# Spectral mixing and a SwiGLU block on one core: the head of the first batch rearranged

## The chip, the core and the metric

The kernel runs on one core of a Trainium2 chip. The core has five engines that follow instruction streams of their own: TensorE (PE in the profile, with PEld for its weight loads), VectorE (DVE), ScalarE (ACT), GpSimd (POOL) and SyncE (SP), which here only issues DMA transfers. The metric is the device time of one execution in microseconds.

## The reference

For each of 8 batches the input x (3008 tokens by 256 channels, float32) is filtered in the frequency domain along the tokens, and the result goes through a SwiGLU block whose weights come as float64:

```python
X = np.fft.rfft(x, axis=1)
F = (filt_r + 1j * filt_i)[None, :, :]
y = np.fft.irfft(X * F, n=x.shape[1], axis=1).astype(np.float32)
x = y.reshape(B * S, D)                      # 24064 x 256
g = x @ w_gate                               # w_gate, w_val: 256 x 1536
silu = g * (1.0 / (1.0 + np.exp(-g)))
out = (silu * (x @ w_val) @ w_out).astype(np.float32)   # w_out: 1536 x 256
```

## The kernel before

**Spectral part.** 3008 = 47 x 64, and the transform is taken in two factors, as matrix products with tables of cosines and sines. `stage1` transforms over 47, `stage2a` over 64 (24 frequencies s in 12 pieces u of two, `N_TWO`); VectorE multiplies by the filter, GpSimd adds the two parts of the complex product, and `stage2b` transforms back over 64. `stage3` transforms back over 47 and leaves the tokens as matrix y. Between `stage2b` and `stage3` the data go through HBM (`d2`, tile d in the profile), since the partitions must be regrouped. `stage3` works on four chunks k of 8 of the first 32 positions; each chunk needs 96 rows (24 frequencies x 4), of four positions in each of two pieces i. `load_t4` reads these rows back.

**Block part.** A step is one chunk k with one third g of the hidden width. `SCHEDULE` is an order, written out by hand, of tokens for all engines: Q and P are products with y, A, B and E are products of sums of y (tile y_t, `combine_sequence`) with sums of weights, which save multiplications; f and c are copies of a product's bank by ScalarE, x and y combine two banks on VectorE, D is a difference on GpSimd, h is the gated product, S are sums of h on GpSimd, W are the products with w_out (banks wF, wA, wG). A bank's later product waits until earlier readers have done: P1 follows f1, P0 follows f0.

**Weights.** They come as float64 and are turned into float32 by the kernel, in 36 halves of 128 x 256 values. `round_half(i)` is a generator that does one half in small instructions: mantissa bits (L403), exponent bits (L406), mantissa to float (L408), exponent with its bias taken off and clamped (VectorE L412 and L415 for i < 8, ScalarE L419, L421, L423 for later ones), sign and exponent joined (L426), low word added (L430), and GpSimd multiplies the two (L438, or L450 and L451). Halves 0 to 7 are w_val and w_gate for g = 0; 8 to 11 are w_out for it, of which four halves make the two sets j = 0 and 1, each finished by four differences on GpSimd (L329). `combine_weights` makes the sums of weights for one pair of blocks: A on VectorE, for some pairs a scaling on ScalarE (L472), then B and E.

**The planner.** `Preparation` gives each of these small instructions a tick, and `tick(step, n)` issues the next n ticks at that place of the program. A half begins 4 ticks after the one before it, but half 8 begins 12 ticks after half 7. `finish(step)` issues what the step needs. In the first step 11 ticks come at places of `SCHEDULE` after A01, in later ones 20.

**The head.** Before the first step the kernel runs batch 0's spectral part by itself, in a loop over u in which `stage2b` trails `stage2a` by `lag` pieces; matmuls named idle, on a tile of zeros or on weights, stand in its gaps. `stage2b`'s result goes from its bank by a ScalarE copy into one of four buffers g and by DMA to `d2`; piece u + 4 needs the buffer of u, so its copy waits until that store has landed. Pieces 0 to 7 are stored by SP's queue, 8 to 11 by ScalarE's. The rows of chunk 0 go into the tile f0, in two loads for each half i; those of the last piece do not go through HBM: eight small transfers bring them straight from g to f0 (L923). The instructions of each engine keep the order of the program (`pin`), so a waiting one holds up all behind it on its engine.

The sums of the weights for g = 0 end with B on GpSimd, and E on VectorE for four of the six pairs.

Of the kernel before, what the change touches and what calls it, by code (L numbers as in the profile page):

```python
# [48 lines left out]
B, S, C = 8, 3008, 256  # L49
# [5 lines left out]
NS, NQ = 24, 64  # L55
NR = 2 * N1
NK = 4 * NS
# [67 lines left out]
def dft_tables():  # L125
# [26 lines left out]
    d[0, :, :, 1] = (-sn * sg).transpose(0, 2, 1)  # L152
    d[1, :, :, 1] = (c * sg).transpose(0, 2, 1)
    d = d.reshape(128, NS, 128)
    de = np.stack([d, d.transpose(2, 1, 0)], 2)

    hi = 2 * np.pi * (np.outer(2 * n1 + 1, s) % (2 * N1)) / (2 * N1)
    scale = np.where(s == 0, 1.0, 2.0) / S
# [45 lines left out]
def kernel(  # L204
# [168 lines left out]
        return spot if i < N_LENT and spot < 3 else None  # L373

    N_EARLY = 12

    def load_weights(i):
        if i in raws or i >= len(weights):
# [9 lines left out]
    def round_half(i):  # L388
# [19 lines left out]
        pin(nc.scalar.activation(out=w, in_=man, func=AF.Copy, scale=2.0 ** -20, bias=1.0))  # L408
        yield
        pf = pw.bitcast(FP32)  # L410
        if i < 2 * len(BLOCKS):
            pin(v.tensor_scalar(out=pf, in0=pw, scalar1=-896.0, scalar2=0.0,  # L412
                                op0=ALU.add, op1=ALU.max))
            yield
            pin(v.tensor_scalar(out=pw, in0=pf, scalar1=255.0, scalar2=2.0 ** 23,  # L415
                                op0=ALU.min, op1=ALU.mult))
            yield
        else:
            pin(nc.scalar.activation(out=pf, in_=pw, func=AF.Relu, bias=off_t))  # L419
            yield  # L420
            pin(nc.scalar.activation(out=pf, in_=pf, func=AF.Relu, bias=top_t, scale=-1.0))  # L421
            yield
            pin(nc.scalar.activation(out=pw, in_=pf, func=AF.Copy, scale=-(2.0 ** 23),  # L423
                                     bias=255 * 2.0 ** 23))
            yield
# [34 lines left out]
    def combine_weights(g, i, j):  # L460

        d = j - i
        wt_f = weights_of(0, 0, g).rearrange("p s z f -> p s (z f)")
        m = wt_f[:, SLOT[f"A{i}{j}"]]
        ui, uj, yi, yj = [wt_f[:, SLOT[f"{p}{q}"]] for p in "PQ" for q in (i, j)]
        if d == 1:
            pin(negated_sum(m, ui, uj))
        else:
            pin(add(nc.vector, m, ui, uj))
        yield  # L470
        if d > 1:
            pin(nc.scalar.mul(m, m, -1.0 / d))  # L472
        yield
        pin(sub(nc.gpsimd, wt_f[:, SLOT[f"B{i}{j}"]], yi, m))
        early = g == 0 and PAIRS_USED.index((i, j)) < 4
        pin(add(nc.vector if early else nc.gpsimd, wt_f[:, SLOT[f"E{i}{j}"]], yj, m))

    def keep_weights(g, piece):

# [7 lines left out]
    class Preparation:  # L487
# [3 lines left out]
        def __init__(self):  # L491
            self.at, self.held = 0, []

            self.ticks, self.need = {}, {}
            base, ready = [], {}

            def put(t, f, by, pool=False):
                self.ticks.setdefault(t, ([], []))[pool].append(f)
                self.need[by] = max(self.need.get(by, 0), t)

            for i, (_, (use, *at)) in enumerate(weights):
                hid, g = use == "hid", at[0] if use == "hid" else at[0] // JB
                by = ((0, 3, 6) if hid else (1, 4, 7))[g]
                b = base[-1] + (4 if i != 2 * len(BLOCKS) else 12) if i else 0
                if i >= N_EARLY:
                    same = [n for n in range(N_EARLY, i) if spot_of(n) == spot_of(i)]
                    k = 2 if spot_of(i) is None else 1
                    last = base[same[-k]] + 8 if same[k - 1:] else 0
                    b = max(b, last + 8)
                    put(max(last, b - 10), lambda i=i: load_weights(i), by)  # L510
                base.append(b)
                if hid and g == NG - 1:
                    ready.setdefault(NT, b)
                half = []
# [6 lines left out]
                times = (0, 1, 2, 3, 4, 6, 7, 9, 10) if i >= 2 * len(BLOCKS) else \  # L521
                    (0, 1, 2, 3, 4, 6, 9, 10)
                for t in times:
                    put(b + t, go, by, t > 8 or t == 7)
                if hid and at[1:] == [BLOCKS[-1], 1]:
                    for n, pair in enumerate(PAIRS_USED):
                        c = combine_weights(g, *pair)
                        for t in range(3):

                            put(b + 11 + n + t, lambda c=c: next(c, None),  # L530
                                by if g or n < 4 else 1, t == 2)
            self.barriers = sorted((t, step) for step, t in ready.items())
            self.end = max(self.ticks)
# [57 lines left out]
    class Spectral:  # L591


        def __init__(self, b):
            self.b = b
            self.d1, self.d2 = [dram_tiles[2 * (b % 2) + i] for i in range(2)]
            self.d1_rows = self.d1.rearrange("a (h n) c -> (a h) n c", h=2)

            self.d2_tokens = self.d2.rearrange("a n c -> (a n) c").rearrange(
                "(n a) c -> n a c", n=N2)  # L600
            self.d2_rows = self.d2.rearrange("a (h n) c -> (a h) n c", h=2)
# [51 lines left out]
        def load_tables(self, i):  # L653
# [5 lines left out]
            for u in range(i * n // NV, (i + 1) * n // NV):  # L659
                self.tb[u], self.f[u] = tb0[:, ts(u, NV)], f0[:, ts(u, NV)]  # L660

        def load_t4(self, k, i, part=None):
            if part is not None:

                t = f0[0:NK, ts(i, NH), :]
                r = (slice(0, 64), slice(64, NK - 4 * NV))[part]
                self.load(out=t[r], in_=self.d2_rows[r, ts(i, NH), :])
            else:
                t = t4pool.tile([128, NH, C], FP32, name=f"t4_{self.b}_{k}_{i}", tag="t4")
                at = 2 * k + i  # L670
                if self.b == 0:
                    self.load(out=t[0:NK], in_=self.d2_rows[:, ts(at, NH), :])
                else:

                    rows = self.d2_tokens.rearrange("(h n) a c -> h (n a) c", h=2)
# [233 lines left out]
        def stage2b(self, u):  # L909
# [8 lines left out]
            if self.b == 0 and u == N_TWO - 1:  # L918
                for i in range(NV):
                    pin(nc.scalar.copy(out=g[:, i], in_=ps[:, i]))  # L920
                for j in range(4 * NV):
                    i, at = j // 4, 64 * (j // 2 % 2) + 32 * (j % 2)
                    pin((nc.scalar, nc.sync)[j % 2].dma_start(  # L923
                        out=f0[4 * NV * u + j:4 * NV * u + j + 1, 0:2 * NH],
                        in_=g[at:at + 2 * NH, i:i + 1]))
            else:
                pin(nc.scalar.copy(out=g, in_=ps))
            queue = nc.scalar if self.b or u >= 8 else nc.sync
            if self.b == 0:
                pin(queue.dma_start(out=self.twos(self.d2, u), in_=g))  # L930
                return
            rows = self.d2_tokens.rearrange("n (p s) c -> (n p) (s c)", p=2)
            pin(queue.dma_start(out=rows[:, ts(u, NV * C)], in_=g.rearrange("q s c -> q (s c)")))
# [243 lines left out]
    with tc.tile_pool(name="start", bufs=1) as spool0:  # L1177
# [45 lines left out]
        idle(zero, [bank("idle") for _ in range(2)], 512)  # L1223
        preparation.tick(0, 5)
        spec.real_part(0)
        lag = 4
        for u in range(N_TWO + lag):
            if u < N_TWO:
                spec.turn(u + 2)
# [16 lines left out]
                for i in range(8, N_EARLY):  # L1246
                    load_weights(i)
            if u == N_TWO - 1:
                for i in range(2):
                    spec.load_t4(0, i, 0)  # L1250
        for i in range(2):
            spec.load_t4(0, i, 1)
        for i in range(2):
            spec.load_t4(1, i)
        preparation.finish(0)
        preparation.tick(0, 4)

        idle(zero, [bank("idle") for _ in range(4)], 512)
        for p in ("A13", "A01"):
# [6 lines left out]
            following.load_x(u)  # L1266
    for d in (2, 1):
        combine_sequence(spec.y[0], d, va=nc.vector)

    def keep_y(k):  # L1270
        pin(nc.sync.dma_start(out=y_dram[k], in_=cur.y[k]))
# [207 lines left out]
```

## Time and profile before

| | |
|---|---|
| time, median of 3 runs | 2827.3 us (2824.12 to 2830.31) |
| span of the profiled execution | 2826.7 us |
| granted TensorE clock, mean | 0.998 |
| PE busy in 60 to 80 us | 13.74 of 20 us |
| PE busy in 80 to 100 us | 18.97 of 20 us |
| PE busy in 100 to 120 us | 17.92 of 20 us |
| PE busy in 120 to 140 us | 20.00 of 20 us |
| POOL busy in 100 to 120 us | 19.69 of 20 us |

A view by windows gives each engine's busy time in a stretch. A view by waits tells what ended an engine's idle time. Between 28 and 100 us its longest entries are these (engine, line waited at, what ended it: us in total, times, longest):

```profile
POOL wt_t L329 <- ACT wt_t L472: 8.6, 1, 8.6
DVE wt_t L326 <- ACT wt_t L472: 6.0, 1, 6.0
ACT wt_t L472 <- DMA f<-x: 4.6, 1, 4.6
ACT x L927 <- DMA d<-x: 4.5, 4, 2.4
```

The first three are one wait seen from three engines: GpSimd and VectorE want a scaled sum of weights, ScalarE has still to make it, and it stands behind the small transfers f<-x that ScalarE's queue issues. The fourth is the wait for a free buffer g.

A few names of tiles: wpb and wpc are the banks of `stage2a` and `stage2b`, wpd those of `stage3` for chunk 0 (pd for later chunks), wk the banks of P and Q, wa and we those of A and B, E, wt_t holds the weights of the hidden part, wo_t those of w_out, pw and w are a half in work.

### The profile page before, as it was taken

The page shows a single profiled execution, that of the slowest core. Times are in us where ns is not written, and L with a number is a line of the kernel's source. Part 1 is how long each engine was busy: PE and PEld are TensorE (multiplying, and loading weights), DVE is VectorE, ACT ScalarE, POOL GpSimd, SP SyncE. Part 2 cuts the span into 40 slices and gives each one's busy share as a digit, 9 for nine tenths or more (in the row PEclk, how much of TensorE's full clock was granted, in tenths as well). Part 3 has the DMA queues.
Part 4 walks back from the last instruction along what each step waited for, and adds up shares of the span by engine and source line. Part 5 has one row for each costly group of instructions (what it writes and reads, how often), then busy time and mean ns, then how long its engine had stood idle before and what let it go on. Part 6 is the DMA issues. An engine that isn't in the chain of part 4 may idle for free.

```text
span 2826.7 us, 48513 instructions
## 1 busy us (share of the span) xinstructions
PE 2786.0 (99%) x15444; PEld 2318.8 (82%) x15444; DVE 1993.1 (71%) x4567; ACT 1564.5 (55%) x4182; POOL 1578.1 (56%) x1683
## 2 busy tenths in 40 slices
PE   8999999999999999999999999999999999999998
PEld 6877878788888888888888888888888888888887
DVE  7898766767667766677766677667676767666666
ACT  5775445555555555555555555555555555555554
POOL 4886575465545654456644566444665455545544
PEclk9999999999999999999999999999999999999999
DMA  9687866877666776667666676667766777654543
GB/s 238 210 275 248 274 215 213 281 221 235 192 184 203 246 221 180 198 212 237 218 185 197 214 242 205 186 192 233 230 207 178 217 222 226 194 149 151 152 137 82
DMA packets 363477, 586.59 MB, mean 208 GB/s; under 512 B 198444, under 2 KB 246380, under 8 KB 363128
## 3 DMA queue, kind: packets, MB, share of 16 engines
q1 hardware_dynamic: 337962, 534.70, 60.9%
q10 hardware_dynamic: 23470, 45.46, 5.9%
q0 software_dynamic: 1792, 3.34, 0.4%
q8 instruction: 125, 2.05, 0.3%
q14 instruction: 128, 1.05, 0.1%
HBM read 467.81 MB, written 101.34 MB: 201 GB/s over the span
## 4 chain that ended last, share of the span: by engine, by line
PE 88%; POOL 3%; DVE 1%; issue 1%; DMA 1%; ACT 0%; ACTq 0%; SPq 0%; POOLq 0%; DVEq 0%
PE wa L1050 24%; PE wk L1050 16%; PE wA L1147 16%; PE we L1050 12%; PE wG L1147 8%; PE wF L1147 4%; PE pd L953 3%; PE wqa L700 2%; PE wqc L759 1%; PE wqb L771 1%; POOL out_dram L1132 1%; POOL h L329 1%; POOL y_t L326 0%; DMA lent<-later_tbl 0%; POOL h L326 0%
## 5 line engine op out<-in xcount | busy, mean ns | idle before, releaser
L1050 PE MATMUL wa<-y_t,wt_t 128*128 128x188 f32 x4464 | 879.5, 323 | 6.1 <-DMA y_t<-yt 1.9
L1050 PEld LDWEIGHTS wa<-y_t,wt_t 128*128 128x128 f32 x4464 | 747.2, 190 | 83.1 <-ACT wa L1076 10.8
L1050 PEld LDWEIGHTS wk<-y,wt_t 128*128 128x128 f32 x2976 | 496.6, 191 | 110.8 <-issue 33.4
L1050 PE MATMUL wk<-y,wt_t 128*128 128x188 f32 x2976 | 573.5, 326 | 5.0 <-DVE y L326 2.8
L326 POOL TENSOR_TENSOR h<-h 128x376 f32<-128x376 f32 x190 | 183.3, 986 | 694.5 <-DVE h L1097 694.5
L329 POOL TENSOR_TENSOR h<-h 128x376 f32<-128x376 f32 x572 | 558.8, 998 | 15.4 <-DVE h L326 15.2
L1147 PE MATMUL wA<-h,wo_t 128*128 128x376 f32 x1532 | 552.3, 483 | 3.6 <-DVE o L326 3.5
L1050 PE MATMUL we<-y_t,wt_t 128*128 128x188 f32 x2232 | 431.8, 323 | 0.7 <-ACT we L1081 0.7
L329 POOL TENSOR_TENSOR D<-f,f 128x376 f32<-128x376 f32 x288 | 279.8, 986 | 258.6 <-ACT f L1065 258.5
L329 DVE TENSOR_TENSOR we<-we,m 128x376 f32<-128x376 f32 x576 | 319.4, 555 | 136.5 <-PE we L1050 70.1
L1050 PEld LDWEIGHTS we<-y_t,wt_t 128*128 128x128 f32 x2232 | 369.5, 190 | 1.5 <-ACT we L1081 1.2
L1147 PEld LDWEIGHTS wA<-h,wo_t 128*128 128x128 f32 x1532 | 275.5, 190 | 113.3 <-issue 6.2
L1085 ACT COPY m<-wa 128x376 f32<-128x376 f32 x576 | 272.6, 473 | 103.0 <-PE wa L1050 100.2
L333 DVE SCALAR_TENSOR_TENSOR y<-wk,c 128x376 f32<-128x376 f32 x480 | 244.4, 539 | 61.4 <-ACT c L1069 39.0
L1092 ACT ACTIVATE g<-wa 128x188 f32<-128x188 f32 x576 | 187.6, 326 | 165.8 <-PE wa L1050 155.3
L1092 ACT ACTIVATE u<-we 128x188 f32<-128x188 f32 x576 | 188.2, 327 | 160.1 <-DVE we L329 153.3
L1147 PE MATMUL wG<-h,wo_t 128*128 128x376 f32 x768 | 274.0, 479 | 0.0
L1069 ACT COPY c<-wk 128x376 f32<-128x376 f32 x288 | 136.4, 473 | 224.8 <-PE wk L1050 189.2
L1065 ACT ACTIVATE f<-wk 128x376 f32<-128x376 f32 x288 | 140.4, 488 | 171.1 <-PE wk L1050 124.3
L1081 ACT COPY we<-y 128x376 f32<-128x376 f32 x480 | 222.2, 480 | 19.6 <-DVE h L1097 13.9
L1097 DVE TENSOR_TENSOR h<-wa,g 128x188 f32<-128x188 f32 x576 | 198.5, 345 | 37.1 <-ACT g L1092 36.8
L1097 DVE TENSOR_TENSOR h<-we,u 128x188 f32<-128x188 f32 x576 | 197.5, 344 | 26.6 <-ACT u L1092 15.6
(165 smaller groups left out, 3515.5 us busy)
## 6 DMA issues: line engine op xcount, KB each, us to landing
wt_t<-w_all SPq DMA_DIRECT2D x174, 896.0 KB
wt_t<-w_all SPq DMA_DIRECT2D x174, 768.0 KB
lent<-filter SPq DMA_DIRECT2D x36, 1024.0 KB
lent<-d SPq DMA_DIRECT2D x84, 256.0 KB
d<-lent ACTq DMA_DIRECT2D x84, 256.0 KB
d<-lent ACTq DMA_DIRECT2D x96, 192.0 KB
lent<-raw SPq DMA_DIRECT2D x144, 128.0 KB
t<-d SPq DMA_DIRECT2D x112, 128.0 KB
```

Of the source, the lines that this page charges most:

```text
L326: return eng.tensor_tensor(out=dst, in0=a, in1=b, op=ALU.add)
L329: return eng.tensor_tensor(out=dst, in0=a, in1=b, op=ALU.subtract)
L333: return nc.vector.scalar_tensor_tensor(out=dst, in0=a, scalar=-1.0, in1=b, op0=ALU.mult, op1=ALU.subtract)
L953: pin(nc.tensor.matmul(out=rows, lhsT=self.t4[k, i][:, j, ts(cb, 128)], rhs=cols, start=j == 0, stop=True, skip_group_check=True))
L1050: pin(nc.tensor.matmul(out=ps[:, z], lhsT=self.wt[:, SLOT[p], z], rhs=rhs, start=start and z == 0, stop=True, skip_group_check=True))
L1065: pin(act.mul(self.small(f"f{i}", f"f{i}", 1), t[f"k{i}"], -1.0))
L1069: pin(act.copy(out=self.small(f"c{i}", f"c{i}", 1), in_=t[f"k{i}"]))
L1081: pin(act.copy(out=self.bank(f"e{at}"), in_=t[f"y{at}"]))
L1085: pin(act.copy(out=self.small(f"m{at}", "m", 4), in_=t[f"a{at}"]))
L1092: pin(act.activation(out=self.small(op, "g", 3, 1)[:, 0], in_=ps[:, 1], func=AF.Silu))
L1097: pin(v.tensor_tensor(out=dst, in0=ps[:, 0], in1=g, op=ALU.mult))
L1147: pin(nc.tensor.matmul(out=self.tiles[at], lhsT=wo_t[:, JB * q + i, WO[p], :], rhs=self.hs[i][:, HID[p]], start=start and i == 0, stop=Tru ...
```

## The change

It concerns batch 0 alone, and there what comes before and in the first step. Six edits:

- the columns of the table for `stage2b` are permuted, so that its rows come out in the order of the chunks, 32 rows for each chunk;
- pieces 8 to 11 are therefore stored in two parts: the 32 rows of chunk 0 at once, by ScalarE's queue, the other 96 (`rest`) by SP's after chunk 0 has been read. The eight direct transfers are dropped; chunk 0 is now read in two loads, of frequencies 0 to 15 and 16 to 23;
- `lag` is 3 instead of 4;
- halves 5, 6 and 7 have their exponents done by ScalarE (`N_SHORT` = 5);
- B and E of all six pairs for g = 0 are on VectorE;
- half 8 begins 20 ticks after half 7 instead of 12, the last two pairs' sums come 3 ticks later, and instead of 4 ticks ahead of `stage3` of chunk 0 there are 10 ticks after the sums of y.

They are to shorten the way from the last piece to the first product with weights, and to take work off GpSimd there.

```diff
-    de = np.stack([d, d.transpose(2, 1, 0)], 2)
+    chunks = np.arange(128).reshape(2, 2, NCHUNK, NW).transpose(2, 0, 1, 3).ravel()
+    de = np.stack([d, d.transpose(2, 1, 0)[:, :, chunks]], 2)
...
+    N_SHORT = 5
...
-        if i < 2 * len(BLOCKS):
+        if i < N_SHORT:
             pin(v.tensor_scalar(out=pf, in0=pw, scalar1=-896.0, scalar2=0.0,
                                 op0=ALU.add, op1=ALU.max))
...
-        pin(sub(nc.gpsimd, wt_f[:, SLOT[f"B{i}{j}"]], yi, m))
-        early = g == 0 and PAIRS_USED.index((i, j)) < 4
-        pin(add(nc.vector if early else nc.gpsimd, wt_f[:, SLOT[f"E{i}{j}"]], yj, m))
+        e = nc.gpsimd if g else nc.vector
+        pin(sub(e, wt_f[:, SLOT[f"B{i}{j}"]], yi, m))
+        pin(add(e, wt_f[:, SLOT[f"E{i}{j}"]], yj, m))
...
-                b = base[-1] + (4 if i != 2 * len(BLOCKS) else 12) if i else 0
+                b = base[-1] + (4 if i != 2 * len(BLOCKS) else 20) if i else 0
...
-                            put(b + 11 + n + t, lambda c=c: next(c, None),
+                            put(b + 11 + n + t + 3 * (n > 3 and not g), lambda c=c: next(c, None),
...
+        def rows(self, t, k, s, n):
+
+            self.load(out=t.rearrange("p (o n) c -> p o (n c)", o=1),
+                      in_=self.d2_rows[k, s, :, n].rearrange("s a n c -> s a (n c)"))
+
         def load_t4(self, k, i, part=None):
             if part is not None:
 
-                t = f0[0:NK, ts(i, NH), :]
-                r = (slice(0, 64), slice(64, NK - 4 * NV))[part]
-                self.load(out=t[r], in_=self.d2_rows[r, ts(i, NH), :])
+                a, e = ((0, 16), (16, NS))[part]
+                self.rows(f0[4 * a:4 * e, 0:NW], k, slice(a, e), slice(0, NW))
...
             if self.b == 0 and u == N_TWO - 1:
                 for i in range(NV):
                     pin(nc.scalar.copy(out=g[:, i], in_=ps[:, i]))
-                for j in range(4 * NV):
-                    i, at = j // 4, 64 * (j // 2 % 2) + 32 * (j % 2)
-                    pin((nc.scalar, nc.sync)[j % 2].dma_start(
-                        out=f0[4 * NV * u + j:4 * NV * u + j + 1, 0:2 * NH],
-                        in_=g[at:at + 2 * NH, i:i + 1]))
...
-                pin(queue.dma_start(out=self.twos(self.d2, u), in_=g))
+                q = 128 if u < 8 else 4 * NW
+                pin(queue.dma_start(out=self.d2_parts[0:q, ts(u, NV)], in_=g[0:q]))
+                if q < 128:
+                    self.rest.append((u, g))
...
-        lag = 4
+        lag = 3
...
             if u == N_TWO - 1:
-                for i in range(2):
-                    spec.load_t4(0, i, 0)
-        for i in range(2):
-            spec.load_t4(0, i, 1)
+                spec.load_t4(0, 0, 0)
+        spec.load_t4(0, 0, 1)
+        for u, g in spec.rest:
+            spec.load(out=spec.d2_parts[4 * NW:, ts(u, NV)], in_=g[4 * NW:])
         for i in range(2):
             spec.load_t4(1, i)
         preparation.finish(0)
-        preparation.tick(0, 4)
...
     for d in (2, 1):
         combine_sequence(spec.y[0], d, va=nc.vector)
+    preparation.tick(0, 10)
```

More of the change, by code (lines that the diff above doesn't have):

```diff
@@ L519, in go @@
                     next(half[0], None)
-                times = (0, 1, 2, 3, 4, 6, 7, 9, 10) if i >= 2 * len(BLOCKS) else \
+                times = (0, 1, 2, 3, 4, 6, 7, 9, 10) if i >= N_SHORT else \
                     (0, 1, 2, 3, 4, 6, 9, 10)
@@ L600, in __init__ @@
                 "(n a) c -> n a c", n=N2)
-            self.d2_rows = self.d2.rearrange("a (h n) c -> (a h) n c", h=2)
+            flat = self.d2.rearrange("a n c -> (a n) c")
+            self.d2_parts = flat.rearrange("(s q) c -> q s c", q=128)
+            self.d2_rows = flat.rearrange("(s k a n) c -> k s a n c", k=NCHUNK, a=4, n=NW)
+            self.rest = []
             self.x, self.t2, self.f, self.tb, self.p, self.t4, self.y = {}, {}, {}, {}, {}, {}, {}
@@ L660, in load_tables @@
                 self.tb[u], self.f[u] = tb0[:, ts(u, NV)], f0[:, ts(u, NV)]
+        def rows(self, t, k, s, n):
+            self.load(out=t.rearrange("p (o n) c -> p o (n c)", o=1),
+                      in_=self.d2_rows[k, s, :, n].rearrange("s a n c -> s a (n c)"))
         def load_t4(self, k, i, part=None):
             if part is not None:
-                t = f0[0:NK, ts(i, NH), :]
-                r = (slice(0, 64), slice(64, NK - 4 * NV))[part]
-                self.load(out=t[r], in_=self.d2_rows[r, ts(i, NH), :])
+                a, e = ((0, 16), (16, NS))[part]
+                self.rows(f0[4 * a:4 * e, 0:NW], k, slice(a, e), slice(0, NW))
+                for i in range(2):
+                    self.t4[k, i] = f0[0:NK, ts(i, NH), :]
+                return
             else:
@@ L671, in load_t4 @@
                 if self.b == 0:
-                    self.load(out=t[0:NK], in_=self.d2_rows[:, ts(at, NH), :])
+                    self.rows(t[0:NK], k, slice(0, NS), ts(i, NH))
                 else:
```

## The prediction, made before the changed kernel had run

> **What bounds the kernel now.** I read the page first. TensorE carries the span, so elsewhere an edit counts only where it moves TensorE; the DVE, ACT and POOL shares are averages.
>
> ```profile
> PE 2786.0 (99%) x15444; PEld 2318.8 (82%) x15444; DVE 1993.1 (71%) x4567; ACT 1564.5 (55%) x4182; POOL 1578.1 (56%) x1683
> ```
>
> The edits all lie before the second step of batch 0, so next I read busy time in windows of 2 us. Columns: busy us of PE, PEld, DVE, ACT, POOL; clock; DMA share; GB/s. TensorE stands idle at 65 to 67 and 74 to 76, and then runs at half clock.
>
> ```profile
> 64.00:66.00 2.00, 0.61 (x2) 0.00 (x0) 0.00 (x0) 0.00 (x0) 0.00 (x0) 1.00 0.78 247
> 74.00:76.00 2.00, 0.00 (x0) 0.00 (x0) 1.35 (x4) 1.42 (x4) 0.33 (x1) 0.99 0.82 190
> 76.00:78.00 2.00, 1.18 (x4) 1.18 (x5) 1.44 (x5) 1.89 (x6) 0.00 (x0) 0.50 0.03 9
> 82.00:84.00 2.00, 2.00 (x12) 1.89 (x11) 1.01 (x2) 0.54 (x2) 2.00 (x2) 0.80 1.03 399
> ```
>
> Then the timeline (start, duration, instruction, idle before and its releaser) tells why.
>
> ```profile
> 62.05 4.17 ACTq L923 DMA_DIRECT2D f<-x  x4
> 66.94 0.42 ACT L472 ACTIVATE wt_t<-wt_t 128x256 f32<-128x256 f32 x1 [4.64 <-DMA f<-x]
> 67.40 0.81 SPq L606 DMA_DIRECT2D f<-d  x2
> 70.21 3.78 PE L956 MATMUL wpd<-wi_t,f 96*128 96x94 f32 x32 [0.63 <-PE widle L588]
> 74.52 0.51 ACT L419 ACTIVATE pw<-pw,off_t 128x256 f32<-128x256 uint32 x1 [1.12 <-DVE pw L406]
> 75.92 0.83 ACT L968 COPY y<-wpd 128x376 f32<-128x376 f32 x2
> 78.22 2.29 POOL L326 TENSOR_TENSOR y_t<-y_t 128x376 f32<-128x376 f32 x2 [3.89 <-DVE y_t L326]
> 81.44 0.48 ACT L1065 ACTIVATE f<-wk 128x376 f32<-128x376 f32 x1 [0.83 <-PE wk L1050]
> 83.91 0.88 PE L1050 MATMUL wa<-y_t,wt_t 128*128 128x188 f32 x4
> ```
>
> The last rows of chunk 0 reach SBUF for the product at 70.21. Its results are evicted only at 75.92: ACT is in order, and eleven weight instructions stand ahead, the last of them waiting for DVE. The second factor (f1, done at 81.92) frees the bank for P1 and P0, and A13 follows at 83.91.
>
> [...] the 128x256 weight addition takes 0.42 with POOL idle and 0.95 beside it, and a 0.41 us instruction waited out a POOL sum.
>
> ```profile
> 59.91 0.42 DVE L326 TENSOR_TENSOR wt_t<-wt_t 128x256 f32<-128x256 f32 x1
> 68.60 0.95 DVE L326 TENSOR_TENSOR wt_t<-wt_t 128x256 f32<-128x256 f32 x1
> 96.64 0.98 POOL L326 TENSOR_TENSOR y_t<-y 128x376 f32<-128x376 f32 x1 [2.38 <-PE we L1050]
> 96.69 1.21 DVE L430 SCALAR_TENSOR_TENSOR w<-wo_t,w 128x256 f32<-128x256 uint32 x1
> ```
>
> [...] Here 2.8 us of idling (74.0 to 76.8) sufficed once, and about 6.8 us at half followed (76.8 to about 83.6, from the clock column).
>
> [...]
>
> **Part by part.**
>
> *Halves 5 to 7 on ScalarE.* DVE loses six instructions at 26.1 to 32.6 (about 2.8 us as they stand), ACT gains nine of about 0.5. DVE can start the spectral multiplies up to 1 us before 32.96, its floor being the copy on POOL (30.96 + 1.47). On the path: nothing. The tail is paced by ACT's evictions, each behind the landing of an earlier store (58.38 waits for a DMA), and the loads ahead of these stay.
>
> *Trail of three.* One more store goes ahead of the 1 MB of w_out loads, one trailing product fewer is left at the end. ACT from 58.38 needs four copies of about 0.6 and three issues of 0.38: 62.3 before, I take 62.0. Hidden behind those landings otherwise.
>
> *Rows by chunks, split stores.* The eight direct copies (62.05 to 67.3 on two queues) go. Instead: a 64 KB store, the load behind it. The last full store, issued at about 58.1, let its reader issue at 60.90, 2.8 later for 256 KB; I take 2.4 from issue for a quarter: 64.4. The old last load took 2.8 from the first of two issues to the product; one issue is 0.4 less[...]: 2.7. First product W at 67.1 (66.2 to 68.2), against 70.21: 3.1 earlier. The four deferred stores (768 KB) and the loads of chunk 1 behind them should land near 72.6; the product that reads them could start at W + 4.7 = 71.8. It waits 0.8, but what follows waits longer below.
>
> *Sums of weights on DVE.* POOL loses eight (4.43 + 0.90 + 0.78 + 0.90 = 7.0 us), DVE gains eight at a pitch of 0.34 with POOL idle, 2.7. Twelve weight operations stand before y, done by about 65 while rows are in flight: hidden.
>
> *Ten ticks moved behind y's sums.* Evictions now begin at W + 1.15 = 68.3, 7.6 earlier. But y needs all four banks (3.8 us of product), so POOL's first sum starts at W + 5.4 = 72.5, 5.7 earlier. Behind DVE's y sums stand 11 weight instructions, and in ACT's queue, ahead of f0 and f1, seven that wait on them. POOL's four sums (0.98, 0.98, 1.37, 1.37 by their rows) run just then. Taking turns as at 67 to 72 (a turn lengthened POOL's instruction by about 0.15), POOL ends at W + 5.95 + 4.7 + 0.45 = W + 11.1; DVE gets four in between and the sixth, half 8's exponent bits, done at W + 12.0. From it ACT needs 3.6 to the end of f1 (pitches 0.54, 0.54, 0.32, 0.35, 0.5, 0.45, 0.45, 0.48): W + 15.6 = 82.7, against 81.92: **0.8 later**. With no waiting it would be W + 5.95 + 6 x 0.34 + 3.6 = W + 11.6 = 78.7. I take turns, because the same operations did so in this trace; both ends go into the range.
>
> *What waits behind.* P1, P0, A13 and all later products queue on TensorE behind f1. P3 ends near 75.5, so TensorE idles about 7 us and resumes at half clock. As long a half-clock stretch as before costs 3.4; before lost 0.35 of this after f1 (83.91 - 81.92, against 1.65 for P1 and P0 at full). Net **3.05 later**.
>
> *POOL's order in step 0.* j = 0's four w_out differences (1.99 us) sat in an idle stretch at 92.3. They now follow y_1's first sums, ahead of y_1's other sums and the last product of half 11, for which TensorE waits already:
>
> ```profile
> 104.81 0.82 POOL L438 TENSOR_TENSOR wo_t<-wo_t,pw 128x256 f32<-128x256 f32 x1
> 105.69 0.90 PE L1147 MATMUL wF<-h,wo_t 128*128 128x376 f32 x2 [1.68 <-POOL wo_t L438]
> ```
>
> So wF moves by **2.1 later**. From step 1 on both programs list the same order: before reaches its need of tick 62, after the same work at 70.
>
> Sum: 0.8 + 3.05 + 2.1 = 5.95 later, 2827.3 + 5.95 = **2833**.
>
> **The rivals.** *The earlier eviction carries through.* For it: TensorE begins the first Q0 at W + 3.8 = 70.9 instead of 76.82 (5.9), and if f1 comes early there is no half-clock stretch (2.6 more on the P and Q products). Against: ACT's seven instructions ahead of f0. With the 2.1 of POOL: 2827.3 - 5.9 - 2.6 + 2.1 = 2821.
>
> *The lock costs little.* f1 at 78.7 (3.2 earlier), TensorE idle for 3.2 and one cold window of 3.4 (loses 1.7 - 0.35), POOL 2.1: 2827.3 - 3.2 + 1.35 + 2.1 = 2827.5. For it: POOL's sums may not meet all the DVE instructions; against: the pairs above.
>
> *Two cold stretches.* The warming matmuls end near 63.7 and the product starts at 67.1: 3.4 us of idling. If that halves the clock, the product takes 3.8 more, and everything behind y with it: 2837. Against: 64.6 to 67.4 did not trip it before.
>
> **How the numbers follow.** Forecast 0.42 at 2833 (spread 2830 to 2837; three in five of it above the 2833 that 0.2% makes, since landings and clock can come out dearer by more than cheaper), little lock 0.24 at 2827.5, carried eviction 0.22 at 2821, two cold stretches 0.12 at 2837. Slower: 0.26 + 0.12 = 0.38; within: 0.16 + 0.24 = 0.40; faster: 0.22. The range takes in most of the cheap and the dear end: 2820 to 2838.
>
> **What would show it.** Right: first wpd product near 67, L968 within 1.5 us of it, then DVE weight instructions of 0.8 or more beside POOL's y_t sums, f1 near 82.7, the clock column at 0.5 behind it, and wF waiting about 3.8 for wo_t. Wrong: f1 before 79, or a full clock at 78 to 86 (carried eviction); a first product after 69 (my DMA latencies); wF released by something else (POOL's order). If TensorE's idle time in later steps shrinks, the head's loss was absorbed, and the total is nearer no change.

## The result, and the profile after

The changed kernel takes 2838.7 us (median of 4 runs, 2837.7 to 2841.2), the kernel before in the same comparison 2826.8: 11.9 us slower, ratio 1.0043 with a 95% interval of 1.0025 to 1.0060. The forecast had the direction, at half the size: 2833, with a range that ended at 2838.

TensorE's busy time grew by 4.6 us and the span by 10.6, so more than half of the loss is idle time:

```profile
PE 2790.6 (98%) x15444; PEld 2324.2 (82%) x15444; DVE 1994.2 (70%) x4569; ACT 1568.2 (55%) x4191; POOL 1571.9 (55%) x1675
```

The windows of 2 us, with the columns of the prediction's windows, show two idle stretches of TensorE, at 68 to 71 and 84 to 89, and half a clock from the first of them to 95:

```profile
68.00:70.00 2.00, 0.10 (x1) 0.00 (x0) 0.00 (x0) 0.00 (x0) 0.00 (x0) 1.00 0.83 161
72.00:74.00 2.00, 2.00 (x12) 2.00 (x11) 0.00 (x0) 0.47 (x1) 0.00 (x0) 0.50 0.21 71
80.00:82.00 2.00, 2.00 (x10) 2.00 (x10) 2.00 (x3) 0.00 (x0) 2.00 (x2) 0.50 0.75 188
84.00:86.00 2.00, 0.00 (x0) 0.00 (x0) 2.00 (x4) 0.42 (x1) 1.34 (x1) 0.50 1.02 393
94.00:96.00 2.00, 2.00 (x14) 2.00 (x13) 0.28 (x2) 0.69 (x2) 0.45 (x1) 0.73 0.00 0
```

In the first stretch every engine is idle: all wait for the rows. In the second VectorE and GpSimd are busy. The timeline has the causes (start, duration, instruction, idle before and its releaser):

```profile
60.81 6.56 SPq L611 DMA_DIRECT2D f<-d  x2
...
66.22 1.88 PE L590 MATMUL widle<-wt_t 128*128 128x512 f32 x4
...
71.32 7.11 PE L966 MATMUL wpd<-wi_t,f 96*128 96x94 f32 x32 [3.22 <-issue]
73.35 0.47 ACT L978 COPY y<-wpd 128x376 f32<-128x376 f32 x1 [8.29 <-PE wpd L966]
...
79.28 1.21 DVE L327 TENSOR_TENSOR y_t<-y 128x376 f32<-128x376 f32 x2
...
79.98 2.47 POOL L327 TENSOR_TENSOR y_t<-y_t 128x376 f32<-128x376 f32 x2 [20.16 <-DVE y_t L327]
80.41 1.20 DVE L334 SCALAR_TENSOR_TENSOR wt_t<-wt_t 128x256 f32<-128x256 f32 x1
...
82.65 1.46 DVE L405 TENSOR_SCALAR wo_t<-wo_t 128x256 uint32<-128x256 uint32 x1
82.76 0.42 ACT L474 ACTIVATE wt_t<-wt_t 128x256 f32<-128x256 f32 x1 [4.41 <-DVE wt_t L327]
...
89.03 0.49 ACT L1075 ACTIVATE f<-wk 128x376 f32<-128x376 f32 x1
...
89.57 2.88 PE L1060 MATMUL wk<-y,wt_t 128*128 128x188 f32 x8 [5.62 <-ACT f L1075]
```

The two loads of chunk 0's rows are issued at 60.81 and 66.61 and the product starts at 71.32, at half clock: 7.11 us instead of 3.78. Its first eviction follows at 73.35, so ScalarE holds nothing up there any more. But then come the ten ticks: while GpSimd sums, VectorE takes 1.2 to 1.6 us for each instruction, ScalarE waits 4.41 us for one of them, f1 ends at 89.52, and P1 has waited 5.62 us for it.

The same product, matched by its place on TensorE in both traces, shows where the loss arises. How much later it starts than before, in us:

| product | later | of it new |
|---|---|---|
| first of chunk 0 (wpd) | 1.1 | 1.1 |
| last of chunk 0 | 4.3 | 3.2 (half clock) |
| Q0 | 1.4 | -2.9 (before waited here for its evictions) |
| P1, behind f1 | 7.1 | 5.7 (wait for f1) |
| second product of A, at 86.8 before | 9.7 | 2.5 (half clock) |
| first wA, behind wF | 11.3 | 1.6 (wait for a weight at wF) |
| at 357 | 12.1 | 0.8 |

In the profiled run of before TensorE ran at half clock once more, from 550 to 554, in that of after it did not; from there on the two traces differ by 9.7 instead of 12.1. The medians differ by 11.9.

### The profile page after: what moved, and what is told of

The parts are those of the page before. It is cut to its first block, busy times and chain, and to the rows that moved or that the text cites. A ratio compares the mean times of both kernels' runs of the same rounds, so it can differ in the third digit from the quotient of the medians.

```text
span 2837.3 us, 48503 instructions
## 1 busy us (share of the span) xinstructions
PE 2790.6 (98%) x15444; PEld 2324.2 (82%) x15444; DVE 1994.2 (70%) x4569; ACT 1568.2 (55%) x4191; POOL 1571.9 (55%) x1675
## 4 chain that ended last, share of the span: by engine, by line
PE 88%; POOL 3%; DVE 1%; issue 1%; ACT 0%; DMA 0%; ACTq 0%; POOLq 0%; SPq 0%; DVEq 0%
PE wa L1060 24%; PE wk L1060 16%; PE wA L1157 16%; PE we L1060 12%; PE wG L1157 8%; PE wF L1157 4%; PE pd L963 3%; PE wqa L712 2%; PE wqc L771 1%; PE wqb L783 1%; POOL out_dram L1142 1%; POOL h L330 1%; POOL D L330 0%; POOL y_t L327 0%; POOL h L327 0%
## 5 line engine op out<-in xcount | busy, mean ns | idle before, releaser
L1060 PEld LDWEIGHTS wk<-y,wt_t 128*128 128x128 f32 x2976 | 497.9, 191 | 113.5 <-issue 33.4
L330 DVE TENSOR_TENSOR we<-we,m 128x376 f32<-128x376 f32 x576 | 319.5, 556 | 136.3 <-PE we L1060 69.6
L1091 ACT COPY we<-y 128x376 f32<-128x376 f32 x480 | 222.2, 480 | 19.4 <-DVE h L1107 13.7
```

Of the source, the lines that this page charges most:

```text
L330: return eng.tensor_tensor(out=dst, in0=a, in1=b, op=ALU.subtract)
L1060: pin(nc.tensor.matmul(out=ps[:, z], lhsT=self.wt[:, SLOT[p], z], rhs=rhs, start=start and z == 0, stop=True, skip_group_check=True))
L1091: pin(act.copy(out=self.bank(f"e{at}"), in_=t[f"y{at}"]))
```

## Experiments

Each is compared with runs of the kernel before on its own chip (medians 2826.2 to 2827.1). The times are medians; the last four columns come from one profiled execution of each kernel, in us from its start. f1 is its end, A13 the start, wA the first product behind wF; in the kernel before these are at 81.92, 83.91 and 108.59, with the first product of chunk 0 at 70.21.

| kernel | time, us | ratio to before, interval | first product | f1 | A13 | wA |
|---|---|---|---|---|---|---|
| after | 2838.7 | 1.0043 (1.0025 to 1.0060) | 71.3 | 89.5 | 92.2 | 119.9 |
| ticks_back | 2827.3 | 1.0005 (0.9997 to 1.0013) | 71.8 | 83.2 | 84.6 | 109.3 |
| lag4 | 2837.3 | 1.0038 (1.0024 to 1.0052) | 72.2 | 90.4 | 93.1 | 120.8 |
| ten_after_f1 | 2839.4 | 1.0046 (1.0034 to 1.0059) | 73.1 | 85.0 | 91.8 | 122.9 |
| ten_before_sums | 2832.7 | 1.0023 (1.0013 to 1.0032) | 71.6 | 85.4 | 88.1 | 116.3 |
| tbs_two | 2830.9 | 1.0012 (1.0006 to 1.0019) | 71.4 | 85.2 | 86.6 | 113.5 |
| before_ten | 2833.7 | 1.0028 (1.0019 to 1.0037) | 69.9 | 84.0 | 86.7 | 117.4 |
| rows_only | 2829.4 | 1.0013 (1.0007 to 1.0020) | 72.5 | 83.9 | 85.4 | 110.0 |
| after_warm | 2836.6 | 1.0035 (1.0022 to 1.0047) | 70.8 | 85.7 | 88.4 | 119.0 |
| tb_warm | 2829.2 | 1.0008 (1.0000 to 1.0016) | 72.2 | 82.9 | 85.7 | 110.4 |
| tb_late_rest | 2832.2 | 1.0020 (1.0012 to 1.0029) | 69.4 | 85.2 | 87.8 | 113.6 |
| before_f1 | 2828.5 | 1.0006 (1.0000 to 1.0013) | 70.2 | 79.9 | 83.3 | 108.3 |
| before_spread | 2828.1 | 1.0006 (0.9998 to 1.0015) | 72.5 | 84.3 | 85.9 | 111.9 |
| spread_more | 2827.2 | 1.0001 (0.9993 to 1.0010) | 69.6 | 76.0 | 77.4 | 106.3 |
| tb_twelve | 2834.0 | 1.0028 (1.0019 to 1.0038) | 70.0 | 85.5 | 87.2 | 110.5 |
| tb_twelve_warm | 2834.0 | 1.0024 (1.0014 to 1.0033) | 71.7 | 87.5 | 89.4 | 112.7 |

### Which edit is it

**ticks_back**: the changed kernel with the sixth edit undone.

```diff
-                b = base[-1] + (4 if i != 2 * len(BLOCKS) else 20) if i else 0
+                b = base[-1] + (4 if i != 2 * len(BLOCKS) else 12) if i else 0
-                            put(b + 11 + n + t + 3 * (n > 3 and not g), lambda c=c: next(c, None),
+                            put(b + 11 + n + t, lambda c=c: next(c, None),
         preparation.finish(0)
+        preparation.tick(0, 4)
...
-    preparation.tick(0, 10)
```

> The changed kernel with its sixth edit undone: half 8 again 12 ticks after half 7, the late sums not shifted, four ticks ahead of stage3, none behind the sums of y. Theory 1 (the block of weight instructions between y and f1 is the main loss): VectorE is idle from 68 to 77 in the changed kernel, so the instructions are done there; f1 follows the last P3 product at about 84.5 instead of 89.5, TensorE's idle stretch of 5.6 us is gone, and the time is 2831 to 2834. Theory 2 (the half clock from 71 on is the main loss, the block only fills time that the slow clock leaves): less than 2 us won, 2837. Theory 3 (the late rows are the loss): the first product stays at 71.3, and the time at 2838.

2827.3, better than theory 1 had it: 11.4 us of the 11.9 are gone. The rows come no earlier (first product at 71.80), the clock is halved from 72 on for 10.2 us, and still wA is only 0.7 later than before. VectorE does the weight instructions while all wait for the rows, at 0.42 and 0.28 each, and goes on to y with none in between:

```profile
68.19 0.28 DVE L408 TENSOR_SCALAR pw<-wo_t 128x256 uint32<-128x256 uint32 x1
68.39 0.41 DVE L330 TENSOR_TENSOR wt_t<-wt_t 128x256 f32<-128x256 f32 x1
...
77.13 0.35 DVE L327 TENSOR_TENSOR y<-wpd,y 128x188 f32<-128x188 f32 x1 [6.44 <-PE wpd L966]
```

**before_ten**: the sixth edit alone, on the kernel before.

```diff
-                b = base[-1] + (4 if i != 2 * len(BLOCKS) else 12) if i else 0
+                b = base[-1] + (4 if i != 2 * len(BLOCKS) else 20) if i else 0
-                            put(b + 11 + n + t, lambda c=c: next(c, None),
+                            put(b + 11 + n + t + 3 * (n > 3 and not g), lambda c=c: next(c, None),
-        preparation.tick(0, 4)
...
+    preparation.tick(0, 10)
```

> The kernel before with the sixth edit alone: half 8 at 20 ticks, the late sums 3 ticks later, no four ticks ahead of stage3, ten behind the sums of y. If the sixth edit is the loss by itself: L968 early (about 71.7), f1 at 88 to 90, A13 at 92, the time 8 to 11 us above before: 2835 to 2838. If the loss needs the late rows and the half clock of the changed kernel as well: at most 4 us above before, 2827 to 2831.

6.6 above before: between the two expectations. The edit is a loss by itself, with the product at full clock and f1 only 2.1 later (14.1 us after the first product); then A13 is 2.8 later and wA 8.8. The other 4.8 of the 11.4 need the other edits as well.

**lag4**: a trail of four in the changed kernel.

```diff
-        lag = 3
+        lag = 4
```

> The changed kernel with a trail of four again, nothing else. Theory 3 (the trail of three makes ScalarE wait 3.8 us for a store at 49 to 53, TensorE idles and goes to half clock at 54.4, and all evictions come 2 us late): the last store is issued at about 62.2 instead of 63.98, the first product with wi_t starts at about 69.5 instead of 71.3, no half clock near 54, and the time is 2836.5 to 2837; if TensorE then no longer goes to half clock at 71, 3 us more are won: 2833. Rival (the rows wait for transfers that the trail does not move): first product within 0.4 us of 71.3, time 2838.5.

2837.3, first product at 72.21, not earlier: the trail of three is not the cause. The half-clock stretch at 54 is gone but another lies at 38. Among the kernels with split stores the last product of `stage2b` ends anywhere from 60.7 to 64.1, and the two of them with a trail of four lie in between (62.3 and 62.5), so the 2 us that the theory started from lie within that scatter.

**rows_only**: the first two edits alone, on the kernel before. Against ticks_back these lines are put back:

```diff
-    N_SHORT = 5
+    N_SHORT = 8
-        lag = 3
+        lag = 4
-        e = nc.gpsimd if g else nc.vector
-        pin(sub(e, wt_f[:, SLOT[f"B{i}{j}"]], yi, m))
-        pin(add(e, wt_f[:, SLOT[f"E{i}{j}"]], yj, m))
+        early = g == 0 and PAIRS_USED.index((i, j)) < 4
+        pin(sub(nc.gpsimd, wt_f[:, SLOT[f"B{i}{j}"]], yi, m))
+        pin(add(nc.vector if early else nc.gpsimd, wt_f[:, SLOT[f"E{i}{j}"]], yj, m))
```

> The kernel before with the first two edits alone (rows by chunks, split stores); trail of four, exponents, sums and ticks as before. If the changed route of the rows is itself the slower one: last store issued near 61.5, landed at 64.1, load 4.6 from issue, first product at 68.8 to 69.5, at full or half clock according to the idle stretch ahead of it; f1 near 80.5 to 82; time 2825.5 to 2827.5. If the late product of the changed kernel came from its other edits (trail, exponents, sums): first product at 67 to 68, time 2824 to 2825.

2829.4: the new route of the rows is slower than the direct transfers that it replaces, without any other edit. It costs 3.2 us by this comparison (interval 2 to 6). How much of that is a later first product isn't shown: it is at 72.51 in this one trace, but over all traces it lies from 69.6 to 72.5 with the direct transfers (five kernels) and from 69.4 to 73.1 with the new route (twelve), on average 1 us later.

### Why the ten ticks are dear

**ten_before_sums**: the block ahead of y's sums, everything else as changed.

```diff
+    preparation.tick(0, 10)
     for d in (2, 1):
         combine_sequence(spec.y[0], d, va=nc.vector)
-    preparation.tick(0, 10)
```

> The changed kernel with its ten ticks ahead of the sums of y instead of behind them, so that GpSimd is idle while VectorE does the block; the block still stands ahead of f0 and f1. Theory L (the block is dear because its instructions take turns with GpSimd's four sums: 1.2 to 1.6 us each instead of 0.4): the block's eleven VectorE instructions take 0.28 to 0.42 each, f1 ends 13 to 14 us after the first product instead of 18.2, and the time falls by 4 to 5 us: 2834. Theory B (the block is dear by its own length and place in the queues, with or without turns): f1 no more than 1.5 us earlier against the first product, time 2837 to 2839.

Theory L: 2832.7, 6.0 below the changed kernel. The same instructions, with GpSimd idle:

```profile
79.39 0.42 DVE L334 SCALAR_TENSOR_TENSOR wt_t<-wt_t 128x256 f32<-128x256 f32 x1
79.73 0.42 DVE L327 TENSOR_TENSOR wt_t<-wt_t 128x256 f32<-128x256 f32 x1
80.06 0.28 DVE L405 TENSOR_SCALAR wo_t<-wo_t 128x256 uint32<-128x256 uint32 x1
```

f1 ends 13.7 us after the first product instead of 18.2.

**ten_after_f1**: the block behind f1 in the first step.

```diff
-    preparation.tick(0, 10)
...
             for place, token in enumerate(SCHEDULE):
+                if b == 0 and step == 0 and place == SCHEDULE.index("f1") + 1:
+                    preparation.tick(0, 10)
```

> The changed kernel with its ten ticks not behind the sums of y but behind f1 in the first step. Theory 1 (block): f1 ends near 84.5 instead of 89.5, GpSimd's sums of y run without turns in about 4.9 us, and 5 to 8 us are won less what the later w_out weights cost at wF (0 to 5): 2832 to 2836. Theory 2 (clock): 2837 to 2838. If the first w_out product waits for a weight 5 us or more, the gain is given back: 2838.

f1 is at 85.0 as expected, and nothing is won: 2839.4. The block only moves the wait, since x03 and s13, which A13 needs, now stand behind it on VectorE:

```profile
PE wa L1060 <- DVE wa L1082: 6.3, 3, 4.7
```

**tbs_two**: ten_before_sums with two ticks more in the first step, behind g1 and h0.

```diff
             for place, token in enumerate(SCHEDULE):
+                if b == 0 and step == 0 and place and SCHEDULE[place - 1] in ("g1", "h0"):
+                    preparation.tick(0)
```

> The changed kernel with its ten ticks ahead of the sums of y (as measured at 2832.7), and two ticks more in the first step, one behind g1 and one behind h0, which gives GpSimd the order of the kernel before: the four w_out differences of j = 0 and the multiplication of half 10 ahead of y_1's later sums. If the weights' two ticks of lag cause the longer wait at wF: it waits 1.7 us instead of 3.3, and the products behind it gain 2 to 3 us: 2830 to 2831. Rival (wF waits as long for y_1's sums or for h): 2832 to 2833.

2830.9. The wait at wF (columns: us in total, times, longest) is halved in the traces, while the intervals of the two times still overlap. First ten_before_sums:

```profile
PE wF L1157 <- POOL wo_t L440: 3.3, 1, 3.3
```

then tbs_two:

```profile
PE wF L1157 <- POOL wo_t L440: 1.6, 1, 1.6
```

So the longer wait was the order on GpSimd: with the weights two ticks behind, the four differences of j = 0 and half 10 come among y_1's sums instead of ahead of them. The 3.6 us by which tbs_two is still above ticks_back are the block's own length ahead of f1 (1.9 at f1) and what lies behind it; this wasn't divided further.

### The rows and the clock

**tb_late_rest**: ticks_back with the deferred stores on ScalarE's queue, behind its first eviction of y, and the loads of chunk 1 after them.

```diff
-        for u, g in spec.rest:
-            spec.load(out=spec.d2_parts[4 * NW:, ts(u, NV)], in_=g[4 * NW:])
-        for i in range(2):
-            spec.load_t4(1, i)
...
         for step in (0, 2, 1, 3):
             run(spec.stage3(0, step))
+            if step == 0:
+                for u, g in spec.rest:
+                    pin(nc.scalar.dma_start(out=spec.d2_parts[4 * NW:, ts(u, NV)], in_=g[4 * NW:]))
+                for i in range(2):
+                    spec.load_t4(1, i)
```

> The same without the warming matmuls, and with the four deferred stores and the loads of chunk 1 issued only behind ScalarE's first eviction of y. Theory C (the last load of chunk 0 takes 4.6 us from issue to the product because 768 KB of stores are on the same engines at once): first product 1.5 to 2 us earlier after the load's issue, 3 us instead of 4.6. Rival (the load is slow by itself[...]): within 0.5 us of 4.6. The loads of chunk 1 come 6 us later, so the first product with them waits, and the time is 2828 to 2832.

The rival holds. From the issue of the last load (64.71) to the product (69.40) it is 4.69 us, in the changed kernel 4.71 (66.61 to 71.32):

```profile
64.71 0.76 SPq L611 DMA_DIRECT2D f<-d  x1
...
69.40 4.81 PE L966 MATMUL wpd<-wi_t,f 96*128 96x94 f32 x25 [3.59 <-issue]
```

Without the stores beside it the product comes no sooner; the load is slow by itself. Its packets in the trace begin 1.5 us after the issue and take 2.4 us here and 2.8 in the changed kernel. The time, 2832.2, lies at the upper end of what was expected: the first product of chunk 1 waits 4.4 us for its rows.

**after_warm** and **tb_warm**: four more warming matmuls ahead of `stage3`, in the changed kernel and in ticks_back.

```diff
-            idle(wt_t[:, at:at + 2].rearrange("p s z f -> p (s z f)"), [bank("idle")], 512)
+            idle(wt_t[:, at:at + 2].rearrange("p s z f -> p (s z f)"), [bank("idle") for _ in range(3)], 512)
```

> The changed kernel with four more warming matmuls on weights ahead of stage3, so that TensorE does not idle from 68.1 to 71.3. If the half clock of the first product is worth its 3.3 us: product in 3.8 us, y and f1 3.3 us earlier (86.4), and with them all behind, 2835 to 2836. The idle wait for f1 stays, and with it a half clock behind it. Rival (the block of ten ticks runs on VectorE and ScalarE and takes up what is won): f1 less than 1.5 us earlier, 2838.

> The changed kernel with its sixth edit undone (as measured at 2827.3), and four more warming matmuls ahead of stage3. If the half clock of 10.2 us at 72 to 82 is lost time: product in 3.8 us, f1 near 80.3 instead of 83.5, A13 near 81.9, and the time 3 us less: 2824 to 2825. Rival (the wait at wF, which GpSimd's sums for the next chunk set, takes it up): wF within 1 us, 2826.5 to 2827.5.

In both, the product of chunk 0 runs at full clock in 3.8 us. In after_warm f1 comes 3.9 us earlier, but wA only 0.9 earlier and the time is 2.1 lower: a half clock of 13.7 us from 78 on, a wait of 2.8 for the rows of chunk 1 and the wait at wF take back the rest. tb_warm wins nothing (2829.2): its first product of chunk 1 waits 2.5 us for rows. So taking the half clock away from the first product is worth about 2 of the 11.9 us, and as the intervals of after and after_warm overlap, even that is not clear of noise.

### Looking for a version that beats both

**before_f1**: the kernel before with its four ticks moved behind f1. **before_spread**: the same ticks one by one behind s13, g1, Q2 and h0. **spread_more**: before_spread with half 11's multiplication on VectorE and more warming matmuls. In order:

```diff
-        preparation.tick(0, 4)
...
+                if b == 0 and step == 0 and place == SCHEDULE.index("f1") + 1:
+                    preparation.tick(0, 4)
```

```diff
-        preparation.tick(0, 4)
...
+                if b == 0 and step == 0 and place and SCHEDULE[place - 1] in ("s13", "g1", "Q2", "h0"):
+                    preparation.tick(0)
```

```diff
-            pin(e.tensor_tensor(out=dst[:, ts(l, 2), :], in0=w, in1=pf, op=ALU.mult))
+            late = nc.vector if i == 11 else e
+            pin(late.tensor_tensor(out=dst[:, ts(l, 2), :], in0=w, in1=pf, op=ALU.mult))
...
-        idle(zero, [bank("idle") for _ in range(4)], 512)
+        idle(zero, [bank("idle") for _ in range(6)], 512)
...
-            idle(wt_t[:, at:at + 2].rearrange("p s z f -> p (s z f)"), [bank("idle")], 512)
+            idle(wt_t[:, at:at + 2].rearrange("p s z f -> p (s z f)"), [bank("idle") for _ in range(2)], 512)
```

> The kernel before with one edit: its four ticks ahead of stage3 moved behind f1 in the first step. If the theory holds that weight instructions ahead of y's evictions on ScalarE held up the start (L968 at 75.92 where the product began at 70.21): L968 at about 71.7, f1 at about 79 instead of 81.9, no half clock at 76 to 83 (2.3 to 3.4 us), in all 4 to 6 us faster: 2821 to 2823. Rival (the weight instructions only move behind f1 and hold up the first w_out product, which waits for GpSimd's L438): wF at 105.7 as before, time 2826 to 2827.

> The kernel before with its four ticks moved from ahead of stage3 to four places of the first step, one tick each behind s13, g1, Q2 and h0. Behind f1 in one block they delayed x03 on VectorE and the gain of 2 us at f1 was lost at A13 (83.5). Spread out: f1 near 80.2, A13 near 81.8 instead of 84.2, and if the way to wF is one chain, wF 2 us earlier: 2824 to 2825. Rival (wF is set by GpSimd's sums for the next chunk and the w_out multiplication behind them): A13 earlier, wF within 0.5 us of 105.7, time 2826 to 2827.

> The same with two more edits: the multiplication of half 11 on VectorE instead of GpSimd, and two more warming matmuls on zeros and two more on weights ahead of stage3. If GpSimd's order holds wF and the clock holds the head: full clock from 61 to 110, f1 near 78.5, wF no longer waits 1.7 us for wo_t, and the time is 2821 to 2823. Rival (another wait takes their place, VectorE's h or the next sums of y on GpSimd): under 1.5 us won, 2825 to 2827; if the warming matmuls run past the landing of the rows, up to 1 us lost.

No version is faster than the kernel before. before_f1 wins 2.0 us at f1 and has 0.3 left at wA: y_1's sums on GpSimd still start at 96.35 (96.64 before), when the last part of y_1 has been evicted, and half 11 stands behind them. In before_spread the rows came late (72.45), so it says little on f1. spread_more is 6.5 us ahead at A13 and 2.3 at wA; its trace stays 2.4 to 3.0 ahead up to 306. Then it loses 1.7 at a product of A that waits for a transfer, first the kernel before, then spread_more:

```profile
PE wa L1050 <- DMA y_t<-yt: 1.9, 1, 1.9
PE wa L1051 <- DMA y_t<-yt: 3.5, 1, 3.5
```

It loses about 1.5 more in each of two half-clock stretches at 336 and 380 that the trace of before does not have. Its 13 runs lie from 2823.6 to 2830.0, about the same ground as those of before.

**tb_twelve** and **tb_twelve_warm**: ticks_back with twelve ticks ahead of `stage3` instead of four, without and with the warming matmuls of tb_warm.

```diff
-        preparation.tick(0, 4)
+        preparation.tick(0, 12)
```

> The changed kernel with its sixth edit undone (as measured at 2827.3), but twelve ticks instead of four ahead of stage3, where VectorE is idle from 68 to 77 and ScalarE from 66 to 73. If the late weight instructions load the first step: wF no longer waits 1.7 us for wo_t, VectorE has some 4 us less to do from 84 to 104, and the time falls by 2 to 4 us: 2823 to 2825. Rival (they run past the landing of the rows and hold up the first evictions, or another wait at wF takes over): 2826.5 to 2829.

> The same with four more warming matmuls ahead of stage3, as in the earlier run with them. If the half clock of the first product counts once the weight instructions are out of the way: 2 us below the kernel without them, 2821 to 2823. Rival (the first product of chunk 1 waits for its rows, as it did for 2.5 us in the earlier run with more warming): the same time within 1 us.

Both take 2834.0, above all that was expected of tb_twelve. (The rival for tb_twelve_warm, the same time within 1 us, holds as a number, but not for its reason.) The first product started at 69.95 in tb_twelve and the weight instructions ran past that, so Q0 waited for y:

```profile
PE wk L1060 <- DVE y L327: 5.1, 1, 5.1
DVE w L405 <- DMA wo_t<-in_moe_w_val_dram: 6.7, 1, 6.7
```

The second line is the cause: with twelve ticks VectorE reaches a half whose load is issued at 73.72 or later, waits 6.7 us for it (7.6 in tb_twelve_warm), and y stands behind. So these two runs don't tell what twelve ticks would do with the data already there.

The wait at wF did go (wA only 1.9 late), and another 5 us were lost between 135 and 293; no run looked into the reason.

## Why the prediction was right and wrong

**Evictions no longer held up: right.** The first followed the start of the product by 2.0 us at half clock.

**The first product at 67.1: wrong by 4.2, the step that failed first.** The step had ScalarE done at 62.0, 2.4 for a quarter store and 2.7 for the last load. Measured: the last store is issued at 63.98 (+2.0), the load 2.63 later (+0.2), and the product 4.71 after that (+2.0). The 62.0 came from one trace, and the same point scatters: ScalarE's last copy ends between 61.3 and 65.1 in the twelve traces with split stores, after 63 in ten of them, and between 61.0 and 64.2 in the five with the old route. Why it came late is open.

The last term was mis-sized: the 0.3 us that it allowed for the load's new layout was the author's estimate, which no trace of before showed. In the changed kernel's trace the last load is 32 packets of 8 KB; seven of them start within 0.15 us of each other and the eighth 0.58 us later, against twelve in 0.25 us for the first load with 16 frequencies. A packet of 8 KB took 0.31 us at best and up to 1.75 for the first ones. In the kernel before, the two last loads are 48 packets of 4 KB, the first twelve start within 0.22 us, and one took 0.16 us at best. From the first packet's start to the last one's end it is 2.75 us in the changed kernel and 1.15 in the kernel before, for 256 KB against 192. tb_late_rest shows that the stores beside the load are not in it; how much is due to fewer packets at once and how much to larger ones was not separated.

**TensorE at full clock for the product: wrong, and a rival had it.** "Two cold stretches" named an idle time ahead of the product that halves the clock and costs it 3.8 us; it was 3.2 us of idling and cost 3.3. What was held against it, that the idle time from 64.6 to 67.4 did not halve the clock in the kernel before, did not hold as a reason: in the same trace TensorE kept its full clock through 2.8 us of idling from 64.62 on, and went to half clock in 2.8 us of idling from 73.99 on. What tells the two apart was not shown. Its 2837 is nearest to the time, in part by luck: after_warm takes the cold product away and wins only 2.1.

**The block of ten ticks takes turns with GpSimd: right, and the main loss.** Expected f1 at W + 15.6 with W the first product, measured W + 18.2, of which 3.3 are the slow product. ten_before_sums shows what the turns cost: 4.5 us at f1, 6.0 in the time. Beside GpSimd's sums a 128x256 weight sum with two tensor inputs went from 0.42 to 1.20, and a `tensor_scalar` on uint32, with one tensor input, from 0.28 to 1.46; the lock in the name of one rival is this taking of turns. The forecast set this late f1 against a first product 3.1 us earlier than before, so only 0.8 was left of it; with W 1.1 later than before instead, f1 is 7.6 later: 0.8, the 4.2 by which W was wrong and the 3.3 of the slow product, less 0.7 by which the block was shorter than expected. This 0.8 that became 7.6 is the term of the forecast's sum that failed; the two others, 3.05 and 2.1, came out at 2.1 and 1.6. That W and the clock account for the 6.8 is worked out from one trace; no run has the block with the rows early on the new route.

**TensorE idle, then 6.8 us at half clock, 3.05 later: right in kind, too large, and the stretch wrong.** From f1 to the second product of A it is 2.1 (7.6 to 9.7). The half clock did not begin in this idle time: it had begun at 71.2 and lasted 23.9 us. (The stretch before that the forecast was built on went from 75.97 to 82.79 by the trace's clock records, and not from 76.8 to 83.6.)

**GpSimd's order at wF, 2.1: right**, with 1.6 in the changed kernel's trace. With the block ahead of the sums, two ticks that restore the order win 1.9 in the time. In the changed kernel's view of wF two releasers are named for the same wait, one for the weight load and one for the matmul:

```profile
  POOL wo_t L440: 3.9, 1
  DMA y<-y: 3.3, 1
```

The multiplication L440 ends at 116.93 and the matmul starts at 116.98, so the first is meant.

**Halves on ScalarE, trail of three, sums on VectorE at nothing: not shown dear, not shown free.** With the rows' edits they give ticks_back, 0.8 us from before, and rows_only without them is at 3.2; the intervals overlap.

**From the second step on the same: right**, within 0.8 us up to 550, where the half clock in the trace of before takes back 2.5.

## What to carry to other kernels

Ask of moved work not only what it frees but what it now stands in front of on each in-order engine: weight instructions were taken from where every engine waited for rows and put between y and the first copies that free a bank. VectorE's weight instructions beside GpSimd's sums took up to three to five times their own time here (0.42 to 1.20, 0.28 to 1.46), so such work belongs where GpSimd is idle; but only if its data are there, or the wait for them stands in front of everything, as in tb_twelve. A gain at one point of a chain (2 us at f1, 6.5 at A13) counts only where it is still there at the next wait that another engine sets.

## What the runs showed of the hardware

The half-clock stretches (clock 0.50) that began before 2800 us are, in the trace of the kernel before, 75.97 to 82.79 and 550.42 to 553.83, 6.8 and 3.4 us long; in that of the changed kernel 54.14 to 57.55 and 71.20 to 95.10, 3.4 and 23.9 us long.

**Going to half clock**: idle times of about the same length did not always have the same effect. In the kernel before, 2.8 us of TensorE idling (64.62 to 67.41) left the clock at 1.00, while in the 2.8 us from 73.99 on it was halved at 75.97. A wait of 2.17 us up to 549.00 was followed by half clock at 550.42, one of 2.20 us up to 380.63 was not; in spread_more, where TensorE waits 2.2 us for the same operand near 380, it was. In the changed kernel it was halved at 54.14 and 71.20, at the end of 2.3 and of 3.2 us of idling. In ticks_back TensorE idled for 1.9 us up to 53.60; the four matmuls of `stage2a` at 55.90 then took 1.92 us instead of 1.03. What decides it was not shown.

**Coming back** did not follow at once from work on TensorE. In the changed kernel it was busy from 71.3 to 83.9 but for gaps under 0.2 us, and the clock stayed at 0.50. Most of this time it worked on 96x94 products: the 32 of chunk 0 took 7.11 us, and their weight loads, which overlap them, 6.90. Then it idled for 5.6 us up to 89.57, and the clock was back at 95.10, 5.5 us after the products that follow f1 began. In the kernel before it was back 6.0 us after the first Q0 began (76.82 to 82.79); in ticks_back about 10 us after the first product of chunk 0 (71.80 to about 82). What brings it back was not tried.
